# Retention, expert attention and Fourier mixing in one kernel: a load of attention outputs moved three units later, converted weights loaded ahead of others, and one PSUM ring for two phases

## The chip, the cores and the metric

The kernel runs on one core of a Trainium2 chip. The time is the device time of one execution in microseconds (us), and what counts is the median over several executions. The engines are named as in the profile: PE is the matrix engine (TensorE), PEld its weight loads, DVE the vector engine, ACT the scalar engine, POOL the GpSimd engine, and SP the sync engine, which here issues nearly all DMA transfers.

## What is computed

The reference, cut to its three stages (8 batches, 576 positions, 512 features):

```python
# 1. retention, 8 heads of 64: causal, decaying, no softmax
ret = (scale * q @ k.T) * Dmat            # Dmat[i, j] = gamma[h] ** (i - j) for i >= j, else 0
x = (ret @ v)                             # heads side by side: [B, 576, 512]
# 2. attention with 4 experts; the two best experts of each token count
for e in range(4):
    a = softmax(causal(scale * (x @ wq[e]) @ (x @ wk[e]).T))
    ye = a @ (x @ wv[e]) @ wo[e]
    out += gate_weight(x, e) * ye
# 3. mixing over tokens and channels
theta = out @ w_theta
zr, zi = out * cos(theta), out * sin(theta)
u = out + w_tok_r @ zr + w_tok_i @ zi     # over the 576 positions
result = u + relu(u @ w_ch)
```

## The kernel before, in words

**Precision.** Most products are made of three matmuls each: both operands are split into a high and a low part (`split`, lines 105 to 107: the high part is a copy on ACT, the low part a subtraction on DVE), and `mm3` (lines 100 to 103) adds high times high, high times low and low times high. The weights of stage 3 come in 64-bit floats. Conversion jobs (`convert`, lines 460 to 483), spread over phase 1, turn them into high and low halves and put these into DRAM scratch tensors: `TT` for theta, `TD` for the token mixing, `CD` for the channels.

**Phase 1** is a loop over 80 units and one closing step (lines 653 to 727). A unit is (batch, expert pair, block of 128 rows). Step t computes the scores of unit t (`at_scores`), transposes the probabilities of unit t - 1 (`at_trans`), multiplies finished groups with the values (`at_out`), and in between does the retention and the projections of the next batch, by a table (`SLOTS`). The last ten units and the closing step have a table of their own, `LAST` (lines 57 and 58): at t = 70 the second half of the projection for queries (`Q01`) and the first half of the keys of the last pair (`K10`), at 71 `K11`, at 72 `Q10` and the fused product `F0`, at 73 `Q11` and `F1`, and from 74 on nine token tiles of batches 0 and 1 (`T`). In this phase the order of PE is written out by hand; the other engines and the DMA queues follow an order that the planner makes from dependencies and from the program's order.

**The keys** of a projection go out by four DMAs (`KK<-KN`, line 251), which put both heads' halves where the scores want them.

**Towards phase 2**, at the end of t = 69 (lines 706 to 715), `fuse_load` allots staging buffers and loads, in this order, four pieces of the transposed output weights (`wost<-wot`), four pieces of the output weights (`wost<-wo`), and the four converted theta tiles (`th<-tt`, line 523). Then `load_o(0)` and `load_o(1)` load the attention outputs of batches 0 and 1. Each issues five DMAs on SP, one for `ol` (line 575) and four for the gate weights `og` (line 579, one buffer only), and one multiplication `ol * og` on POOL (line 580). `fuse(p)` (lines 532 to 536) multiplies the output weights with theta: 12 matmuls of 512 columns. `token_tile` (lines 585 to 613) makes from a piece of `ol` the features of 128 tokens and their theta: 24 matmuls of 512 columns into two PSUM tiles (`ps` and `th`), emptied by ACT and DVE. Token tile 0 is the first reader of `load_o(0)`; token tile 4, the tile of both batches' last 64 rows, is the first reader of `load_o(1)`.

**Phase 2** (from line 735) goes over the batches. `mix(b, h)` (lines 742 to 803) multiplies the token weights with the modulated features into four accumulators, 108 matmuls, which DVE empties (line 799, for batch 0 line 801); `channel` and `channel2` (lines 808 to 840) multiply with the channel weights into eight tiles, which DVE empties (line 839 or 824). Between the halves of `mix` the token tiles of later batches are made. The order of PE is the planner's too in this phase.

**PSUM.** Phase 1 has a pool `ps1` with a ring of eight banks (`name="w"`, `WB = 8`). It is released ahead of phase 2, and a pool `ps2` takes the same eight banks: four are fixed by name to the accumulators (`acc00` to `acc11`, one buffer each) and four are a ring `w` for token tiles and channel products. Two accumulator sets at the ends (`spare`) take the ring.

Of the kernel before, what the change touches and what calls it, by code (L numbers as in the profile page):

```python
# [10 lines left out]
F32 = mybir.dt.float32  # L11
# [38 lines left out]
WB = 8  # L50
# [13 lines left out]
def tile_kernel(ctx: ExitStack, tc: tile.TileContext, qk, kv, w1, wo, wot, wd, cst, out):  # L64
# [239 lines left out]
    def work(b, names):  # L304
        for n in names.split():
            x = b + n.islower()
            if x < B:
                if n in "Gg":
                    gate(x)
                elif n[0] == "T":  # L310
                    token_tile(ps1, 0, len(X2))
                elif n[0] == "F":
                    fuse(int(n[1]))
                elif n[0] in "Vv":
                    proj_v(x, int(n[1]))
                else:
                    proj_qk(x, int(n[1]), int(n[0] in "Kk"), int(n[2]))
# [188 lines left out]
    def fuse_load():  # L506

        def put(src, sl, h, l):
            st = wa.tile([128, 256], F32, name="wost", bufs=8)
            nc.sync.dma_start(st, src[:, sl])  # L510
            FP.append((h, l, st))

        for kt in range(4):
            wt = wa.tile([128, 2, 2, C], F32R, name=f"wt{kt}", bufs=1)
            put(wot, slice(kt * 256, kt * 256 + 256), wt[:, 0].rearrange("p a c -> p (a c)"),
                wt[:, 1].rearrange("p a c -> p (a c)"))
            FW.append(wt)
        for g in range(4):
            sl = slice((g % 2) * 256, (g % 2) * 256 + 256)
            put(wo, slice(g * 256, g * 256 + 256), WOH[:, g // 2, sl], WOL[:, g // 2, sl])  # L520
        for kt in range(4):
            th = wa.tile([128, 2, DM], F32R, name=f"th{kt}", bufs=1)
            nc.sync.dma_start(th.bitcast(F32), TT[kt])
            FW[kt] = (th, FW[kt])

    def fuse_split(n):
        while FP[n:]:
# [54 lines left out]
            tc.add_manual_dep(m.ins, MARK["ch"].ins.name, mybir.DependencyInfo(  # L582
                mybir.DependencyClass.Sync, mybir.DependencyReason.DATA), reason="behind the channel products")

    def token_tile(pp, g, i):

        b0 = 2 * g
        oh = wk1.tile([128, 2, C], F32R, name="oh", bufs=2)
        ol = wk1.tile([128, 2, C], F32R, name="oll", bufs=2)
        if i == 4:  # L590
            for w in range(2):
                sl = slice(w * 64, w * 64 + 64)
                split(oh[:, :, sl], ol[:, :, sl], OL[b0 + w][:, :, 512:576])
        else:
            b, m = (b0, i) if i < 4 else (b0 + 1, i - 5)
            split(oh, ol, OL[b][:, :, m * C:m * C + C])
        ps = pp.tile([128, DM], F32, name="w", bufs=WB if pp is ps1 else 4)
        for p in range(2):
            mm3(ps, oh[:, p, :], ol[:, p, :], WOH[:, p, :], WOL[:, p, :], p == 0, p == 1)
        if pp is ps1:  # L600
            th = pp.tile([128, DM], F32, name="w", bufs=WB)
        else:
            th = pp.tile([128, DM], F32, name="w", bufs=4)
        for p in range(2):
            mm3(th, oh[:, p, :], ol[:, p, :], MH[:, p, :], ML[:, p, :], p == 0, p == 1)
        x2 = wk1.tile([128, DM], F32, name="x2", bufs=EARLY)
        nc.scalar.activation(x2, ps, AF.Copy)
        k = wk1.tile([128, DM], F32, name="k", bufs=1)
        nc.scalar.activation(k, th, AF.Copy, scale=1.0 / TWO_PI, bias=MAGIC)
        nc.vector.tensor_scalar(k, k, MAGIC, TWO_PI, op0=OP.subtract, op1=OP.mult)  # L610
        nr = wk1.tile([128, DM], F32, name="nr", bufs=EARLY)
        nc.vector.tensor_sub(nr, k, th)
        X2[g, i], NR[g, i] = x2, nr
# [39 lines left out]
    for t in range(nu + 1):  # L653
        b, k = divmod(t, 10)
        if b < B - 1:
            more, between, after = *SLOTS[k], ""
        else:
            b = B - 1
            more, between, after = LAST[t - 10 * b]
        if t < nu:  # L660
            at_scores(units[t])
            work(b, more)
            if units[t][2] == NCH - 1:
                at_norm(*units[t][:2])
        if t == nu - 1:
            assert not jobs[1]
            cvt.release()
            atk.release()
            zp = pool("zp")
        if between == "O":  # L670
            for o in outs:
                at_out(*o)
            outs = []
        ready, new = outs, []
        if t:
            at_trans(units[t - 1])
            ub, up, um = units[t - 1]
            if GROUPS[GRP[um]][-1] == um:
                new.append((ub, up, GRP[um]))
        outs = new  # L680
        if b < B - 1:
            if between[:1] == "R":
                c = int(between[1])
                x = b + 1
                def mid():
                    for o in ready:
                        at_out(*o)

                ret_step(x, c - 1, mid)
            else:  # L690
                outs = ready + outs
        else:
            work(b, between)
            for o in ready if t < nu else ready + outs:
                at_out(*o)
        work(b, after)


        i = int(t >= JOBS[0])
        x = t - JOBS[0] if i else t - 2  # L700
        while jobs[i] and (x + 1) / due[i] >= njobs[i] - len(jobs[i]) + 1 - 1e-6:
            with ExitStack() as es:
                for e in ("dve", "act"):
                    es.enter_context(tc.issue_after(MARK[e].ins))
                jobs[i].pop(0)()
        if t == nu - 11:
            assert not jobs[0]
            ret.release()
            w2 = pool("w2")
            WOH, WOL, MH, ML = [w2.tile([128, 2, DM], F32R, name=x) for x in ("WOH", "WOL", "MH", "ML")]  # L710
            wol = pool("wol")
            wa = pool("wa")
            fuse_load()
            load_o(0)
            load_o(1)
        if t == nu - 10:
            fuse_split(4)
        if t == nu - 8:
            fuse_split(0)
        if t == nu - 7:  # L720
            w1p.release()
            wa.release()
            w2b = pool("w2b")
            TK = w2b.tile([128, 9, 2, S], F32R, name="TK")
            wk1 = pool("wk1")
            for kt in KORD:
                nc.sync.dma_start(TK[:, kt].bitcast(F32), TD[kt])
# [1 line left out]
        z_tile(0, i, 0)  # L729
    first.close()  # L730
    att.release()
    ps1.release()


    wk = pool("wk")
    CH = wk.tile([128, 4, 2, DM], F32R, name="CH")
    for kt in range(4):
        nc.sync.dma_start(CH[:, kt].bitcast(F32), CD[kt])
    ps2 = pool("ps2", space=PSUM)
    UT = {}  # L740

    def mix(b, h, behind=None):
        g, w = divmod(b, 2)
        tiles = [0, 1, 2, 3, 4] if w == 0 else [4, 5, 6, 7, 8]
        ts = TH if b else TS
        spare = h and b in EDGE
        acc = [[ps2.tile([128, t1 - t0], F32, name="w" if spare else f"acc{d}{i}", bufs=4 if spare else 1,
                         padded_shape=[128, 512]) for i, (t0, t1) in enumerate(ts)] for d in range(2)]
        ks = []
        for i in tiles:  # L750
            if w == 0 or i != 4:
# [56 lines left out]
    def channel2(b, ets):  # L808
# [3 lines left out]
        for h in range(2):  # L812
            for et in ets:
                es = slice(et * C, et * C + C)
                for kt in (2 * h, 2 * h + 1):
                    for j, (t0, t1) in enumerate(TH):
                        if not kt:
                            ps[et, j] = ps2.tile([128, t1 - t0], F32, name=f"acc{et % 2}{j}", bufs=1,
                                                 padded_shape=[128, 512])
                        mm3(ps[et, j], CH[:, kt, 0, es], CH[:, kt, 1, es], uh[:, kt, t0:t1], ul[:, kt, t0:t1],  # L820
                            kt == 0, kt == 3)
                for j, (t0, t1) in enumerate(TH if h else []):
                    o = u[:, et, t0:t1]
                    MARK["ch"] = nc.vector.scalar_tensor_tensor(o, ps[et, j], 0.0, o, op0=OP.max, op1=OP.add)
                    if b == B - 1:
                        nc.sync.dma_start(out[b, et, :, t0:t1], o)
                if h and b < B - 1:
                    nc.sync.dma_start(out[b, et], u[:, et, :])

    def channel(b, et):  # L830
# [1 line left out]
        u = XU[b]  # L832
        es = slice(et * C, et * C + C)
        for j, (t0, t1) in enumerate(TH):
            ps = ps2.tile([128, t1 - t0], F32, name="w", bufs=4, padded_shape=[128, 512])
            for kt in range(4):
                mm3(ps, CH[:, kt, 0, es], CH[:, kt, 1, es], uh[:, kt, t0:t1], ul[:, kt, t0:t1], kt == 0, kt == 3)
            o = u[:, et, t0:t1]
# [30 lines left out]
    for b in range(B):  # L869
# [6 lines left out]
        mix(b, 0)  # L876
        for x in q[:2]:
            if x not in X2:
                token_tile(ps2, *x)
            if b:  # L880
                x_put(*x)
        def put():
# [5 lines left out]
        mix(b, 1, None if b else put)  # L888
        for x in q[2:]:
            if x not in X2:  # L890
                token_tile(ps2, *x)
            if b:
                x_put(*x)
        if 0 < b < B - 1:
# [4 lines left out]
            continue  # L899
        for i in range(2):  # L900
            channel2(b, (2 * i, 2 * i + 1))
    ps2.release()
    wk.release()
    zp.release()
    wk1.release()
# [79 lines left out]
```

## Time and profile before

| | us |
|---|---|
| median of 3 runs | 880.44 |
| lowest and highest | 877.99 and 881.26 |
| profiled execution, its own time | 879.58 |
| its span (first to last instruction) | 877.8 |
| PE busy in the span | 859.2 |

The profile is one execution, taken by the hardware profiler. In a timeline a line has start, duration, engine, line of the kernel, operation, tiles (written <- read), the shape and how many instructions were merged into it; in brackets stands the idle time of the engine before it and what ended it. In a list of waits the numbers are the total in us, how often, and the longest. Matmuls overlap one another, so what PE loses at a place is better read from starts than from the idle time in brackets.

### The profile page before, as it was taken

The numbers are of one execution on the slowest core, as the hardware profiler recorded it, in microseconds if no ns is written. First come the engines' busy times: TensorE is split into PE (matmuls) and PEld (weight loads), VectorE is DVE, ScalarE is ACT, GpSimd is POOL, SyncE is SP. The second block draws the span as 40 slices with busy tenths as digits, with TensorE's granted clock in tenths as the row PEclk, the third lists the DMA queues.
The fourth block names the chain that finished last, engine by engine and source line by source line (L and its number), as shares of the span: only waits on it lengthen the run. The fifth ranks groups of instructions, "written<-read, shape, count | busy, mean of one in ns | idle before, by whom it ended". The sixth has DMA issues, their size and how long they took to land.

```text
span 877.8 us, 25574 instructions
## 1 busy us (share of the span) xinstructions
PE 859.2 (98%) x10072; PEld 795.2 (91%) x10072; DVE 622.0 (71%) x1729; ACT 454.6 (52%) x1258; POOL 218.7 (25%) x268
## 2 busy tenths in 40 slices
PE   6999999999999999999999999999999999999998
PEld 6989889888888989898789999999989999999998
DVE  4588787878788886876678777676377665766632
ACT  1366667666666766666576445353244533444320
POOL 3325253443525453341300012010210103001010
PEclk9899999999999999999999999999999999999999
DMA  9857677676867676548674442422525233241411
GB/s 317 246 155 239 171 221 199 194 224 187 255 169 222 202 211 179 160 108 238 185 265 170 83 111 47 120 37 61 141 57 139 62 96 93 34 124 25 100 34 54
DMA packets 140440, 130.30 MB, mean 148 GB/s; under 512 B 75808, under 2 KB 114976, under 8 KB 140320
## 3 DMA queue, kind: packets, MB, share of 16 engines
q1 hardware_dynamic: 140176, 128.39, 52.6%
q8 instruction: 79, 1.29, 0.6%
q0 software_dynamic: 144, 0.28, 0.2%
q14 instruction: 41, 0.34, 0.1%
HBM read 78.03 MB, written 32.00 MB: 125 GB/s over the span
## 4 chain that ended last, share of the span: by engine, by line
PE 88%; DMA 4%; DVE 3%; ACT 1%; issue 1%; POOL 1%; SPq 0%; ACTq 0%; DVEq 0%; POOLq 0%
PE acc L787 22%; PE w L245 11%; PE w L101 6%; PE w L102 6%; PE w L103 6%; PE w L335 6%; PE w L273 6%; PE w L401 5%; PE w L382 5%; PE w L787 3%; PE w L158 3%; PE w L143 3%; DMA kt<-qk 2%; DMA KK<-KN 1%; PE w L180 1%
## 5 line engine op out<-in xcount | busy, mean ns | idle before, releaser
L787 PE MATMUL acc<-TK,zh 128*128 128x288 f32 (+2 forms) x896 | 156.4, 296 | 0.5 <-ACT ob L405 0.5
L787 PEld LDWEIGHTS acc<-TK,zh 128*128 128x128 f32 x896 | 132.1, 189 | 1.2 <-issue 0.6
L343 ACT ACTIVATE P<-P,st 128x128 f32<-128x128 f32 (+4 forms) x160 | 95.4, 598 | 42.2 <-DVE st L338 41.9
L803 POOL TENSOR_TENSOR ul<-u,uh 128x576 fp32r<-128x576 f32 x16 | 24.2, 1531 | 309.6 <-ACT uh L802 309.6
L787 PE MATMUL acc<-TK,zl 128*128 128x288 f32 (+1 forms) x448 | 95.9, 295 | 0.0
L106 ACT ACTIVATE zh<-cs 128x512 fp32r<-128x512 f32 x64 | 40.3, 630 | 76.6 <-PE acc L787 61.4
L335 PE MATMUL w<-KK,U 128*64 128x288 f32 (+4 forms) x384 | 76.6, 327 | 1.5 <-DMA KK<-KN 1.4
L107 DVE TENSOR_TENSOR zl<-cs,zh 128x512 fp32r<-128x512 f32 x64 | 45.1, 705 | 43.2 <-ACT zh L106 42.5
L338 DVE CUSTOM_DVE_ANT_0 P<-w,cm 128x128 f32<-128x128 f32 (+4 forms) x160 | 71.1, 477 | 4.8 <-PE w L335 3.9
L787 PEld LDWEIGHTS acc<-TK,zl 128*128 128x128 f32 x448 | 72.4, 189 | 0.0
L626 ACT ACTIVATE cs<-cs,quarter 128x256 f32<-128x256 f32 x72 | 36.5, 507 | 55.4 <-DVE cs L624 55.2
L629 DVE SCALAR_TENSOR_TENSOR cs<-cs,x 128x512 f32<-128x512 f32 x72 | 50.7, 706 | 20.1 <-ACT cs L627 19.4
L382 PE MATMUL w<-ident,P 128*128 128x128 f32 (+2 forms) x480 | 60.1, 260 | 1.6 <-DVE sm L147 1.3
L335 PEld LDWEIGHTS w<-KK,U 128*128 128x128 f32 (+1 forms) x384 | 54.0, 171 | 8.0 <-DVE nwt L355 1.5
L193 POOL TENSOR_TENSOR xl<-xt,xh 128x512 fp32r<-128x512 f32 (+1 forms) x40 | 47.8, 1195 | 45.4 <-ACT xh L192 45.4
L479 POOL TENSOR_TENSOR r<-r,ex 128x192 f32<-128x192 f32 (+1 forms) x51 | 29.5, 578 | 116.2 <-ACT hl L480 42.0
L192 ACT ACTIVATE xh<-xt 128x512 fp32r<-128x512 f32 (+1 forms) x40 | 23.5, 589 | 66.9 <-DVE xt L190 66.8
L103 PE MATMUL w<-uh,CH 128*128 128x288 f32 x192 | 56.6, 295 | 0.0
L102 PE MATMUL w<-ul,CH 128*128 128x288 f32 x192 | 56.5, 294 | 0.0
L101 PE MATMUL w<-uh,CH 128*128 128x288 f32 x192 | 56.5, 294 | 0.0
L401 PE MATMUL w<-PT,V 128*64 128x192 f32 (+3 forms) x576 | 56.4, 325 | 0.0
L382 PEld LDWEIGHTS w<-ident,P 128*128 128x128 f32 (+2 forms) x480 | 47.1, 138 | 8.3 <-DVE sm L147 2.7
(153 smaller groups left out, 2340.4 us busy)
## 6 DMA issues: line engine op xcount, KB each, us to landing
KK<-KN SPq DMA_DIRECT2D x128, 144.0 KB
kt<-qk SPq DMA_DIRECT2D x32, 512.0 KB
kv<-kv SPq DMA_DIRECT2D x32, 512.0 KB
raw<-wd SPq DMA_DIRECT2D x43, 192.0 KB
xd<-xb SPq DMA_DIRECT2D x126, 64.0 KB
out<-u SPq DMA_DIRECT2D x28, 288.0 KB
u<-xd SPq DMA_DIRECT2D x28, 288.0 KB
td<-hl SPq DMA_DIRECT2D x27, 192.0 KB
```

The source lines that it names most:

```text
L101: nc.tensor.matmul(ps, ah, bh, start=first, stop=False)
L102: nc.tensor.matmul(ps, ah, bl, start=False, stop=False)
L103: nc.tensor.matmul(ps, al, bh, start=False, stop=last)
L245: nc.tensor.matmul(ps, W[:, kt, w0:w0 + 128], x[:, kt, sl], start=x is xh and W is WH and kt == 0, stop=x is xl and kt == 3)
L273: nc.tensor.matmul(ps[:R], x[:, kt, cs], W[:, kt, w0:w0 + NV], start=x is xh and W is WH and kt == 0, stop=x is xl and kt == 3)
L335: nc.tensor.matmul(ps[s][:R], U[:, s, rs], KK[:, s, x, j0:j1], start=x == 0, stop=x == 1)
L338: MARK["dve"] = nc.vector.tensor_tensor_reduce(Ps[s][:R, j0:j1], ps[s][:R], cm[:R, o + j0:o + j1], 1.0, st[:R, 0, s:s + 1] if i else 3.0e3 ...
L343: MARK["act"] = nc.scalar.activation(Ps[s][:R, :n], Ps[s][:R, :n], AF.Exp, bias=st[:R, last, s:s + 1], scale=-1.0, accum_out=SUM[p][:R, m, ...
L382: nc.tensor.transpose(tp[:w, j, :], Ps[s][:R, j * C:j * C + w], ident[:R, :R])
L401: nc.tensor.matmul(po[s * 64:s * 64 + 64, c0:], V[:ROWS[j], j, 2 * p + s, :], v, start=j == 0, stop=j == last, skip_group_check=True)
L629: nc.vector.scalar_tensor_tensor(z, cs, -1.0, x2[:, None, ds].to_broadcast([128, 2, 256]), op0=OP.mult, op1=OP.mult)
L787: nc.tensor.matmul(acc[d][j], A[:, dc], TK[:, kt, W, t0:t1], start=q == 0 and n == 0, stop=q == 8 and n == 2)
```

## The change

Three things change. In `fuse_load` the four loads of converted theta tiles stand ahead of the four loads of the output weights (the transposed ones stay first). `load_o(1)` leaves the end of t = 69 and stands at the end of t = 72, behind `fuse_split(0)`. And the pool `ps1` with its ring of eight banks lives on through phase 2: all accumulators, channel products and token tiles take the next place of that one ring, and `ps2`, its fixed accumulators and the special cases go.

```diff
@@ fuse_load
-        for g in range(4):
-            sl = slice((g % 2) * 256, (g % 2) * 256 + 256)
-            put(wo, slice(g * 256, g * 256 + 256), WOH[:, g // 2, sl], WOL[:, g // 2, sl])
         for kt in range(4):
             th = wa.tile([128, 2, DM], F32R, name=f"th{kt}", bufs=1)
             nc.sync.dma_start(th.bitcast(F32), TT[kt])
             FW[kt] = (th, FW[kt])
+        for g in range(4):
+            sl = slice((g % 2) * 256, (g % 2) * 256 + 256)
+            put(wo, slice(g * 256, g * 256 + 256), WOH[:, g // 2, sl], WOL[:, g // 2, sl])
@@ token_tile: the pool is no longer an argument
-        ps = pp.tile([128, DM], F32, name="w", bufs=WB if pp is ps1 else 4)
+        ps = ps1.tile([128, DM], F32, name="w", bufs=WB)
...
-        if pp is ps1:
-            th = pp.tile([128, DM], F32, name="w", bufs=WB)
-        else:
-            th = pp.tile([128, DM], F32, name="w", bufs=4)
+        th = ps1.tile([128, DM], F32, name="w", bufs=WB)
@@ the loop over units
             fuse_load()
             load_o(0)
-            load_o(1)
         if t == nu - 10:
             fuse_split(4)
         if t == nu - 8:
             fuse_split(0)
+            load_o(1)
@@ between the phases
-    ps1.release()
...
-    ps2 = pool("ps2", space=PSUM)
@@ mix
-        spare = h and b in EDGE
-        acc = [[ps2.tile([128, t1 - t0], F32, name="w" if spare else f"acc{d}{i}", bufs=4 if spare else 1,
-                         padded_shape=[128, 512]) for i, (t0, t1) in enumerate(ts)] for d in range(2)]
+        acc = [[ps1.tile([128, t1 - t0], F32, name="w", bufs=WB, padded_shape=[128, 512]) for t0, t1 in ts]
+               for d in range(2)]
@@ channel2
-                            ps[et, j] = ps2.tile([128, t1 - t0], F32, name=f"acc{et % 2}{j}", bufs=1,
-                                                 padded_shape=[128, 512])
+                            ps[et, j] = ps1.tile([128, t1 - t0], F32, name="w", bufs=WB, padded_shape=[128, 512])
@@ channel
-            ps = ps2.tile([128, t1 - t0], F32, name="w", bufs=4, padded_shape=[128, 512])
+            ps = ps1.tile([128, t1 - t0], F32, name="w", bufs=WB, padded_shape=[128, 512])
@@ the end
-    ps2.release()
+    ps1.release()
```

## Rows read from the trace of the kernel before

**Rows 1.** The page: the span, and PE's share of it (busy us, instructions).

```profile
span 877.8 us, 25574 instructions
...
PE 859.2 (98%) x10072; PEld 795.2 (91%) x10072; DVE 622.0 (71%) x1729; ACT 454.6 (52%) x1258; POOL 218.7 (25%) x268
```

**Rows 2.** Who waited for whom, PE: us in total, times, longest us.

```profile
PE w L335 <- DMA KK<-KN: 1.4, 1, 1.4
...
PE w L101 <- DMA th<-tt: 0.8, 2, 0.5
...
PE w L101 <- ACT oh L106: 0.7, 1, 0.7
...
PE acc L787 <- ACT ob L405: 0.5, 1, 0.5
PE acc L787 <- DVE u L799: 0.3, 1, 0.3
```

**Rows 3.** Timeline of PE: starts and followers of the two fused products.

```profile
409.22 0.48 PE L101 MATMUL w<-th,wt 128*128 128x512 f32 x1
...
413.56 0.44 PE L401 MATMUL w<-PT,V 128*64 128x128 f32 x4
...
417.13 0.48 PE L101 MATMUL w<-th,wt 128*128 128x512 f32 x1
...
419.97 1.22 PE L335 MATMUL w<-KK,U 128*64 128x288 f32 x8
```

**Rows 4.** Timeline of PE: two score steps over 128 columns and their followers.

```profile
397.73 0.64 PE L335 MATMUL w<-KK,U 128*128 128x128 f32 x4
398.20 0.74 PE L245 MATMUL w<-xh,WH 128*128 128x288 f32 x4
...
426.20 0.44 PE L335 MATMUL w<-KK,U 128*128 128x128 f32 x2
...
428.26 0.45 PE L101 MATMUL w<-WOH,oh 128*128 128x512 f32 x1
```

**Rows 5.** Timelines of PE and DVE where phase 2 begins.

```profile
461.38 1.78 PE L401 MATMUL w<-PT,V 128*64 128x192 f32 x20
463.66 0.89 PE L787 MATMUL acc<-TK,zh 128*128 128x256 f32 x5 [0.49 <-ACT ob L405]
...
463.19 0.69 DVE L107 TENSOR_TENSOR zl<-cs,zh 128x512 fp32r<-128x512 f32 x1
```

**Rows 6.** Timeline of SP (DMA issues): the loads around the change.

```profile
394.77 0.90 SPq L510 DMA_DIRECT2D wost<-wo  x2
...
403.04 2.69 SPq L523 DMA_DIRECT2D th<-tt  x4
...
411.23 2.05 SPq L251 DMA_DIRECT2D KK<-KN  x2
421.51 2.40 SPq L579 DMA_DIRECT2D og<-gd  x4
423.95 3.96 SPq L251 DMA_DIRECT2D KK<-KN  x6
```

**Rows 7.** Timeline of POOL: the multiplications of the two loads.

```profile
418.80 2.68 POOL L580 TENSOR_TENSOR ol<-ol,og 128x1152 f32<-128x1152 f32 x1 [11.15 <-DMA KK<-KN]
426.93 2.64 POOL L580 TENSOR_TENSOR ol<-ol,og 128x1152 f32<-128x1152 f32 x1 [5.45 <-DMA og<-gd]
```

**Rows 8.** Timeline of PE: first matmuls of token tiles 0 and 4.

```profile
421.98 0.50 PE L101 MATMUL w<-WOH,oh 128*128 128x512 f32 x1
...
440.83 0.39 PE L101 MATMUL w<-WOH,oh 128*128 128x512 f32 x1
```

**Rows 9.** Timeline of DVE: a step of token tile 0.

```profile
427.81 2.03 DVE L610 TENSOR_SCALAR k<-k 128x512 f32<-128x512 f32 x1 [0.56 <-ACT k L609]
```

**Rows 10.** Phase 2, PE's second mixing half of batch 1, and DVE's emptying in batch 3.

```profile
533.43 0.54 PE L787 MATMUL acc<-TK,zth 128*128 128x288 f32 x2 [0.28 <-DVE u L799]
...
629.73 1.62 DVE L799 TENSOR_TENSOR u<-acc,u 128x288 f32<-128x288 f32 x4 [1.18 <-PE acc L787]
```

More of the change, by code (lines that the diff above doesn't have):

```diff
@@ L310, in work @@
                 elif n[0] == "T":
-                    token_tile(ps1, 0, len(X2))
+                    token_tile(0, len(X2))
                 elif n[0] == "F":
@@ L583, in load_o, with token_tile @@
                 mybir.DependencyClass.Sync, mybir.DependencyReason.DATA), reason="behind the channel products")
-    def token_tile(pp, g, i):
+    def token_tile(g, i):
         b0 = 2 * g
@@ L878, in tile_kernel @@
             if x not in X2:
-                token_tile(ps2, *x)
+                token_tile(*x)
             if b:
@@ L890, in tile_kernel @@
             if x not in X2:
-                token_tile(ps2, *x)
+                token_tile(*x)
             if b:
```

## The prediction, made before the changed kernel was run

> **What bounds the kernel now.** I read four views, in this order. First the page: PE is busy for 859.2 of 877.8 us [rows 1], so no other engine sets the time over any long stretch, and a change that leaves the matmuls alone, as this one does, can win only what PE spends waiting, 18.6 us in all. Second, PE's list of waits, to see which of these waits the edits touch [rows 2]. Four do belong to them: the wait for key copies (1.4), two waits for theta tiles (0.8), one wait at the first mixing step for ACT's emptying of the last phase-1 bank (0.5), and one wait for DVE's emptying of an accumulator (0.3). Together 3.0 us of idle time: the size of what can happen is a third of a per cent. Third, PE's timeline at each of these places, since a matmul that restarts is longer than one in a run and the loss is more than the idle time. Fourth, SP's and POOL's timelines, for what holds the late transfers.
>
> The reader should see a chain there. SP issues its DMAs in order. It issued two of the four key copies of `K10` at 411.23, and then the gate-weight loads of `load_o(1)` stood at its head; they had to wait, for `og` has one buffer and the first `load_o` multiplies out of it until 418.80 + 2.68 = 421.48. Only at 421.51 did SP go on, and the other two copies of `K10`, with the four of `K11`, went out from 423.95 on [rows 6, 7]. PE did the first two score matmuls at 426.20 and then had to wait [rows 4].
>
> **The change part by part.**
>
> *Theta tiles ahead of output weights.* The fused product F0 takes from 409.22 to 413.56, 4.34 us; F1, the same 12 matmuls with everything there, takes from 417.13 to 419.97, 2.84 us [rows 3]. So the late tiles cost 1.50 us. In the new order the first two theta tiles go out where two pieces of output weights went, at 394.77, and the other two right behind the key and gate transfers, before 403.04 [rows 6]: over 8 us and over 2 us earlier for the last two than they have to be to save 1.5. Gain taken: 1.50, between 0.8 (the idle time alone, [rows 2]) and 1.50. The price is that the output weights come some 2 us later, by their exchange of places with the rest of the theta loads, 2.69 us of issue for four [rows 6]. Their splits feed ACT and DVE at t = 72 and their first reader on PE is token tile 0, at 421.98 [rows 8], some 16 us behind the end of these issues at 405.73. I cost it at nothing; if the cover is gone, ACT's work behind a late split moves by the same 2 us at most.
>
> *`load_o(1)` three units later.* What moves are five DMA issues on SP (four of them 2.40 us together) and one POOL multiplication of 2.64 us [rows 6, 7]. On SP they go behind all eight key copies of `K10` and `K11`, which is the point: the copies of `K10` then follow one another from 411.23 on and land well ahead of PE, and nothing stands behind a waiting `og` load but later work. The score step cost 2.06 us from 426.20 to 428.26; the same step over 128 columns took 0.47 us at 397.73 [rows 4]. Gain 1.59, between 1.4 (the idle time, [rows 2]) and 1.59. The queue is also lighter: without the second `ol` (576 KB by its shape) ahead of the key copies, and with theta gone earlier, the four `og` loads of `load_o(0)` land earlier, and so does its multiplication. That is needed, for token tile 0 starts at 421.98, half a microsecond behind the multiplication's end at 421.48 [rows 7, 8]: if PE comes 1.5 us earlier and the multiplication does not, the first gain is lost at this place. I expect the multiplication some 3 us earlier, because two theta tiles of four, 512 KB each by their shape, are out of its way. What is late next is the second multiplication. Its reader is token tile 4, at 440.83, and by then it has been done since 429.57 [rows 7, 8]; with PE 3.1 us earlier, 8 us of cover are left, more than the three units can eat as long as `og` is waited for only until the first multiplication. On POOL it is moved past conversion work whose results are wanted in phase 2 only: nothing.
>
> *One ring.* At the hand-over the first accumulator waits for ACT to empty the very last phase-1 tile, idle 0.49 [rows 5], since the new pool begins when all of the old one is done. In one ring the accumulators take banks used some tiles before. But PE would then be there at 463.17, and the low part of the first modulated tile ends at 463.19 + 0.69 = 463.88 [rows 5]; four matmuls of high parts come first (of the five in 0.89 us), so about 0.2 of the 0.49 comes back as a wait for DVE. Gain 0.30, between 0.1 and 0.49. In phase 2 the accumulators are no longer fixed by name: the second half of batch 1 has not to wait for the emptying of the first half if four other banks are free, and the idle 0.28 [rows 10] goes: 0.28, between a loss of as much and 0.28. All other crossings in phase 2 show no idle time before, so the ring can win nothing there; what it may lose is the second rival.
>
> Sum: 1.50 + 1.59 + 0.30 + 0.28 = 3.67 us. On the profiled execution's own time, 879.58 (span 877.8 and 1.8 around it), that gives 875.9; the median of the runs shown is 0.86 above that execution, so for a median 880.44 - 3.67 = 876.8, 0.42% less.
>
> *A row against the moved load.* While POOL multiplied from 426.93 to 429.57, DVE's step on token tile 0 took 2.03 us, and it ended at 429.84, just behind POOL [rows 7, 9]. So a DVE instruction that meets this multiplication can last until it is over. The multiplication moves, and it will meet other DVE work; PE's part in it is the third rival. The Trainium skill has this as a rule (SBUF — State Buffer, "Who interferes with whom"): GpSimd and certain vector instructions take the same pair of ports as an exclusive lock, and the one that starts later is held until the first is over. By that rule the moved load would cost the length of one multiplication wherever PE waits for the DVE step that meets it; the trace agrees in that the DVE step ended 0.27 us behind POOL.
>
> **The rivals.**
>
> *One more stall goes.* PE also waits 0.7 us for a split at a token tile of phase 2 [rows 2]. With free banks in any place the planner can order PE's work otherwise and keep it busy there. For: the planner moves whole blocks when a bank is not free. Against: that split waits for a load, not for a bank. Time: 880.44 - 3.67 - 0.7 = 876.1, and a little less where restarts count.
>
> *Reused banks are the freshest.* If the ring hands the next user the bank that was emptied last, PE stands at each crossing from `mix` to the work behind it until DVE has emptied four accumulators, 1.62 us [rows 10], where fixed names gave it other banks. Eight batches have seven such crossings with other work between the halves: 7 x 1.62 = 11.3 us. Against the 3.4 us won elsewhere this ends at 880.44 - 3.4 + 11.3 = 888.3, slower. One bank instead of four, 0.41 each, costs 2.8 and ends at 879.9; slower by over 0.5% needs at least 7.8 us, so it decides from about 1.1 us a crossing. For: nothing in the trace of before shows which bank a shared ring gives. Against: phase 1 works with such a ring of eight, and its waits for banks in the list are small.
>
> *A cover is too short.* Token tile 0 finds the first multiplication undone, or a DVE step that PE waits for meets the second one. The first takes back at most 1.50, the second at most 2.03 [rows 9]: 878.3 to 878.8.
>
> *The move does nothing.* The planner may issue the moved loads as early as before, since they depend on little. If the `og` loads still stand between the key copies, the 1.59 stay lost: 878.4. Against: what stands earlier in the program has gone first on SP whenever it was ready.
>
> **How the numbers follow.** About 0.5%, 4.4 us, is what a measurement of this kernel can tell from no change, that is a time below 876.0 or above 884.8. Forecast as summed 0.52; one more stall goes 0.18; a cover too short 0.14; the move does nothing 0.08; freshest banks 0.08. The forecast, 876.8, is near the bound, and the bounds of its terms (2.0 to 3.9 us) with restarts and the scatter of medians put about 0.15 of its 0.52 below 876.0; with the first rival's 0.18 this makes faster 0.33. Slower is the second rival less its cheap end, 0.07. The rest, 0.60, is within 0.5%. The range leaves out most of the second rival, and on the low side what is more than 3 us beyond the forecast: 873.8 to 880.2.
>
> **What would show it.** In the profile of the changed kernel F0 should take 2.8 us, the score step over 128 columns ahead of token tile 1 about 0.5 us, and SP should show eight key copies without a stop. PE's list of waits should have no line with `th` or `KK`, and the first mixing matmul should wait for DVE's `zl`, if for anything. A wait of PE at token tile 0 for `oh`, or at a crossing in phase 2 for line 799, 839 or 607, would show the cover or the ring to be wrong. The prediction is wrong if PE's total idle time falls by less than 2 us or by more than 6, or if PE's busy time changes with the same matmuls.

## The result: slower by 1%, lost at one place that the prediction had not read

The changed kernel takes 888.10 us (median of 4 executions, 886.92 to 890.84); the kernel before, in the same comparison, 879.22 (4 executions, 876.63 to 881.26). The ratio is 1.0105, 95% interval 1.0076 to 1.0135. Forecast were 876.8 us, a gain, and a range of 873.8 to 880.2: the time lies above the range, and the sign is wrong too.

The page of the kernel after, first its span and busy times, then two rows of its 40 slices, each of 22 us:

```profile
span 886.5 us, 25575 instructions
...
PE 859.4 (97%) x10072; PEld 795.9 (90%) x10072; DVE 623.5 (70%) x1729; ACT 455.9 (51%) x1258; POOL 219.9 (25%) x268
...
PE   7899999999999999999999999999699999999998
...
PEclk9999999999999999999999999999799999999999
```

PE is busy for as long as in [rows 1], with as many matmuls. What grew is its idle time, 886.5 - 859.4 = 27.1 us where 18.6 stood before. One slice, the 29th (620.6 to 642.7 us), falls to 6 tenths and takes the granted clock down with it. PE's list of waits says what it is:

```profile
PE w L101 <- ACT oh L106: 8.5, 1, 8.5
```

The 0.7 us of the same line in [rows 2] have become 8.5. The lines for `KK`, `th`, `ob` at line 787 and the accumulators, the other four of [rows 2], are gone from the list. So all three parts of the change took away what they were to take away, and something else costs more. PE's timeline says where (lines 781, 793 and 797 of the kernel after are lines 787, 799 and 803 of the one before):

```profile
411.44 0.48 PE L101 MATMUL w<-th,wt 128*128 128x512 f32 x1
...
414.37 0.44 PE L401 MATMUL w<-PT,V 128*64 128x128 f32 x4
...
426.78 0.66 PE L335 MATMUL w<-KK,U 128*128 128x128 f32 x4
427.28 0.44 PE L101 MATMUL w<-WOH,oh 128*128 128x512 f32 x1
...
460.41 1.78 PE L401 MATMUL w<-PT,V 128*64 128x192 f32 x20
462.12 1.33 PE L781 MATMUL w<-TK,zh 128*128 128x256 f32 x8
...
628.32 0.43 PE L781 MATMUL w<-TK,zl 128*128 128x288 f32 x2
637.27 0.80 PE L101 MATMUL w<-WOH,oh 128*128 128x512 f32 x1 [8.52 <-ACT oh L106]
...
642.10 0.40 PE L103 MATMUL w<-MH,oll 128*128 128x512 f32 x1
```

The first three pairs answer to [rows 3], [rows 4] and [rows 5]: F0 takes 414.37 - 411.44 = 2.93 us (4.34 before), the score step 0.50 (2.06), the hand-over 1.71 (2.28). The fourth is the loss: the last matmul of the first mixing half of batch 3 starts at 628.45, and the first matmul of the next token tile (the first of batch 4) at 637.27.

With starts of PE at four places the whole execution divides into stages. F0 is the first fused product; mix(0,0) the first matmul of phase 2; mix(3,0) the first half of the mixing of batch 3; ch(3) its channel products. The table has the profiled execution of every kernel of this study (e1 to e10 are below; "ring" is the shared ring of eight banks):

| us | start of F0 | F0 to mix(0,0) | mix(0,0) to mix(3,0) | mix(3,0) to ch(3) | ch(3) to last matmul |
|---|---|---|---|---|---|
| before | 409.22 | 54.44 | 152.41 | 43.44 | 214.17 |
| **after** | 411.44 | 50.68 | 152.07 | **53.47** | 214.17 |
| e1, both moves, no ring | 409.17 | 51.24 | 152.72 | 43.41 | 214.17 |
| e2, ring alone | 407.70 | 54.05 | 152.07 | 53.82 | 214.17 |
| e3, ring, `ul` on DVE | 409.88 | 50.68 | 152.34 | 49.88 | 214.17 |
| e4, ring, tiles later | 410.95 | 50.68 | 152.08 | 42.43 | 214.26 |
| e5, theta alone | 408.66 | 51.59 | 152.73 | 43.44 | 214.17 |
| e6, `load_o(1)` alone | 409.82 | 51.88 | 152.39 | 43.41 | 214.17 |
| e7, ring, input later | 409.74 | 50.68 | 152.38 | 57.41 | 214.17 |
| e8, no ring, input later | 413.43 | 51.24 | 153.01 | 43.85 | 214.29 |
| e9, as e4 | 409.34 | 50.68 | 152.07 | 42.42 | 214.52 |
| e10, no ring, tiles later | 408.66 | 51.31 | 152.97 | 42.40 | 214.37 |

From before to after that is -3.76, -0.34, +10.03 and 0.00, in sum +5.9. The other 2.7 of the 8.65 by which the spans differ are 2.22 at the start, ahead of anything that the change touches there, and 0.5 behind the last matmul. The start of F0 scatters from 407.70 to 413.43 over the kernels of the table (e2 with the ring has the earliest, e8 without it the latest), so I take the 2.22 for scatter of single executions. That isn't shown, and the medians leave it open: they differ by 8.9 us (6.7 to 11.9 by the interval), more than the 5.9 of the stages, and in e3, e4 and e9, which have all three parts of the change too, the medians also lie some 2 us higher against before than the stages behind F0 say (in e7 0.4).

Why PE stands there is told by the chain of waits of the kernel after, from 619.95 on (start, length, engine and line on the chain; "issue" is time in which the engine waited for nothing that the profile shows):

```profile
619.95 8.55 PE w L781 x64
...
628.52 0.64 ACT zh L106
...
629.79 0.83 DVE u L793 x2
...
630.69 0.69 ACT uh L796
...
631.45 0.66 POOL ul L797
...
634.21 2.58 POOL ol L580
...
636.80 0.42 ACT oh L106
...
637.27 0.80 PE w L101
```

The token tile needs `oh`, the high part of `ol`, and `ol` is ready when POOL has multiplied it by the gate weights (line 580). On POOL that multiplication stands behind two subtractions `ul` of batch 3. These need `uh` from ACT, which needs `u`, which DVE makes when the first mixing half is done (and, here, behind a split `zh`, `zl` for the next half). So the token tile behind this half waits, through four engines, for the end of this very half: 8.8 us from start to start, with PE empty.

The chain was there before as well. The timelines of POOL and of PE of the kernel before:

```profile
631.68 2.94 POOL L803 TENSOR_TENSOR ul<-u,uh 128x576 fp32r<-128x576 f32 x2 [41.85 <-ACT uh L802]
634.58 2.67 POOL L580 TENSOR_TENSOR ol<-ol,og 128x1152 f32<-128x1152 f32 x1
```

```profile
636.59 0.42 PE L787 MATMUL acc<-TK,zl 128*128 128x288 f32 x2
637.74 0.50 PE L101 MATMUL w<-WOH,oh 128*128 128x512 f32 x1 [0.73 <-ACT oh L106]
```

POOL ends at 637.25 here too. But PE did other work meanwhile: its mixing matmuls run on from 616.07 to 636.72, 156 of them, where a half has 108. The planner had put 48 matmuls of the *second* half, 6.4 us at 0.133, ahead of the token tile; only 0.7 us of the wait were left. In the kernel after it goes 108, 24, 108, 36: half, two token tiles, half, three token tiles, which is the program's order. (A token tile is 12 matmuls of 512 columns, six into `ps` and six into `th`, not 24 as the section on the kernel says.) The ring took away the work that had covered the chain.

The chain itself also became longer. Counted from the start of the half, POOL ends after 637.25 - 616.07 = 21.2 us before and 636.78 - 614.19 = 22.6 us after. The timeline of DVE of the kernel after:

```profile
629.18 0.69 DVE L107 TENSOR_TENSOR zl<-cs,zh 128x512 fp32r<-128x512 f32 x1 [2.51 <-ACT zh L106]
629.79 1.54 DVE L793 TENSOR_TENSOR u<-w,u 128x288 f32<-128x288 f32 x4
```

The split `zl` of the next half stands ahead of the four emptyings `u`; in the kernel before, `u` went first, at 629.73 [rows 10], and this `zl` at 631.27. So of the 7.8 us that PE stands longer (8.7 against 0.9, from starts), 6.4 are the missing 48 matmuls and 1.4 the longer chain.

Only batch 3 pays. Batches 1 and 5 issue the same pair of loads, but in the kernel after POOL multiplies the first of them at 507.38 and 733.54, ahead of `ul` and 13 us ahead of the token tiles at 520.91 and 747.21. Why the planner put batch 4's multiplication behind `ul`, in both kernels, isn't settled.

### The profile page after: what moved, and what is told of

Its sections match the earlier page's. It is cut to its first block, busy times and chain, and to the rows that moved or that the text cites. A ratio compares the mean times of both kernels' runs of the same rounds, so it can differ in the third digit from the quotient of the medians.

```text
span 886.5 us, 25575 instructions
## 1 busy us (share of the span) xinstructions
PE 859.4 (97%) x10072; PEld 795.9 (90%) x10072; DVE 623.5 (70%) x1729; ACT 455.9 (51%) x1258; POOL 219.9 (25%) x268
## 4 chain that ended last, share of the span: by engine, by line
PE 88%; DVE 4%; DMA 3%; issue 2%; POOL 1%; ACT 1%; SPq 0%; DVEq 0%; ACTq 0%; POOLq 0%
PE w L781 26%; PE w L245 11%; PE w L101 8%; PE w L102 8%; PE w L103 8%; PE w L335 6%; PE w L401 5%; PE w L382 5%; PE w L273 5%; PE w L158 3%; PE w L143 2%; DMA kt<-qk 2%; PE w L180 1%; PE w L173 1%; DMA raw<-wd 1%
## 5 line engine op out<-in xcount | busy, mean ns | idle before, releaser
L781 PE MATMUL w<-TK,zh 128*128 128x288 f32 (+2 forms) x1024 | 178.6, 296 | 0.1
L781 PEld LDWEIGHTS w<-TK,zh 128*128 128x128 f32 x1024 | 150.8, 189 | 0.6 <-DVE u L793 0.3
L781 PE MATMUL w<-TK,zl 128*128 128x288 f32 (+2 forms) x512 | 109.4, 295 | 0.0
L781 PEld LDWEIGHTS w<-TK,zl 128*128 128x128 f32 x512 | 82.9, 189 | 0.0
L103 PE MATMUL w<-uh,CH 128*128 128x288 f32 x256 | 75.4, 295 | 0.0
L101 PE MATMUL w<-uh,CH 128*128 128x288 f32 x256 | 75.4, 295 | 0.0
L102 PE MATMUL w<-ul,CH 128*128 128x288 f32 x256 | 75.4, 295 | 0.0
```

The lines of the kernel that those rows point to most:

```text
L101: nc.tensor.matmul(ps, ah, bh, start=first, stop=False)
L102: nc.tensor.matmul(ps, ah, bl, start=False, stop=False)
L103: nc.tensor.matmul(ps, al, bh, start=False, stop=last)
L781: nc.tensor.matmul(acc[d][j], A[:, dc], TK[:, kt, W, t0:t1], start=q == 0 and n == 0, stop=q == 8 and n == 2)
```

## The experiments

The theories that I set out with: **A**, the ring alone makes the loss, by the order of PE at this one place; **B**, the moved `load_o(1)` makes it, by what it shifts on SP and POOL; **C**, the prediction's slow rival, that the ring hands out freshly emptied banks and each crossing loses a little. For e7 and e8: **P**, one ring shared by accumulators and token tiles keeps PE in the program's order, so nothing can be pulled ahead; **Q**, the planner chose that order for a reason that has nothing to do with the sharing.

### e1: both moves without the ring

```diff
 fuse_load: th<-tt stands ahead of wost<-wo, as in the change
 t == nu - 12:   -            load_o(1)
 t == nu - 8:    +            load_o(1)
```

> The kernel before with the two moved loads and without the one ring. Theory A (the ring alone makes the loss; the moves win what was forecast): some 3.1 us under the kernel before, about 876, both phase-1 waits of PE gone (F0 near 2.9 us, score step near 0.5 us), and PE's wait at the token tile of phase 2 stays near 0.7 us. Theory B (the moved load shifts the order of POOL and SP behind it and so makes the wait in phase 2): PE waits some 8 us for the split of that token tile here too, time 885 or more.

877.35 us (10 executions), 0.9985 of before (0.9967 to 1.0003; before 879.41 in 20). F0 to mix(0,0) falls from 54.44 to 51.24, mix(3,0) to ch(3) stays at 43.41. In its list of waits the lines for `KK` and `th` are gone; the one for `ob` at the hand-over (0.5), which the ring took away, stays, and the one for `oh` at the token tile has the 0.7 us of before. So the moves don't make the loss, against B. What they win shows in the stages (3.2 us up to mix(0,0)); the medians differ by 2.1 us, less than the 3.1 expected, with an interval that takes in no change.

### e2: the ring without the moves

```diff
-    ps1.release()
-    ps2 = pool("ps2", space=PSUM)
+    acc, channel products and token tiles: ps1.tile(..., name="w", bufs=WB)
 loads in the order of before
```

> The one ring alone, loads as in the kernel before. Theory A: PE waits some 8 to 9 us at the first token tile of batch 4, as in the changed kernel, then runs some 10 matmuls at half pace, and with 0.5 to 1 us won at the beginning of phase 2 and in batch 1 the time is 9 to 10 us over the kernel before, 888 to 890; both phase-1 waits are as before. Theory B: no such wait, 878 to 879.

888.82 us (4), 1.0130 of before (1.0104 to 1.0156). Its list of waits has the late loads of before (`KK` 1.4, `th` 1.2) and the stall of after (`oh` 8.5, once) side by side. The ring makes all of the loss: 53.82 us from mix(3,0) to ch(3), and no other stage is longer than before. The time is in the range of A, 888 to 890. A holds so far, and B is out.

### e5 and e6: each move alone

e5 has the new order of theta and output weights only, e6 only `load_o(1)` three units later.

> The kernel before with the theta loads moved ahead and nothing else. If the terms of the sum stand by themselves: F0 takes 2.9 us instead of 4.3, and the score step ahead of token tile 1 still waits for key copies, 2.0 us. If the two gains hang together (token tile 0 stands until the first multiplication of attention outputs is done, as the second load is still in the queue), PE waits some 1 us at token tile 0. No new wait in phase 2.

> The kernel before with the load of batch 1's attention outputs moved and nothing else. F0 still takes some 4.3 us, as theta comes as late as before; the score step takes 0.5 us instead of 2.1. No new wait in phase 2: its wait at the token tile stays near 0.7 us. Theory B (the moved load makes the wait in phase 2) would want 8 us there.

One execution each, 876.46 and 877.55 us (before 880.09 in 9). A single time says little here, since those of before in this comparison run from 875.98 to 882.63; the stages say more. F0 to mix(0,0) gains 2.85 with e5 and 2.56 with e6, together 5.41, where both moves in one kernel (e1) gain 3.20. The gains overlap, against the expectation that each term stands by itself. PE's wait for `oh` at the token tile of phase 2 is 0.7 us in both, against B. The timelines of PE and of POOL of e5:

```profile
411.58 0.44 PE L401 MATMUL w<-PT,V 128*64 128x128 f32 x4
...
424.62 0.41 PE L335 MATMUL w<-KK,U 128*128 128x128 f32 x2 [0.18 <-DMA KK<-KN]
424.87 0.45 PE L101 MATMUL w<-WOH,oh 128*128 128x512 f32 x1
```

```profile
415.44 2.67 POOL L580 TENSOR_TENSOR ol<-ol,og 128x1152 f32<-128x1152 f32 x1 [8.34 <-PE w L382]
```

With theta out of the way the first multiplication starts 6.78 us behind F0's start (408.66), where [rows 3, 7] give 9.58. `og` is free that much earlier, and the key copies behind it come in time for all but 0.18 us: the score step, which began at 424.00, takes 0.87 us instead of 2.06, though `load_o(1)` has not moved. The other way round, PE's timeline in e6:

```profile
409.82 0.48 PE L101 MATMUL w<-th,wt 128*128 128x512 f32 x1
...
412.49 0.50 PE L101 MATMUL w<-th,wt 128*128 128x512 f32 x1 [0.33 <-DMA th<-tt]
413.38 0.44 PE L401 MATMUL w<-PT,V 128*64 128x128 f32 x4
```

Without the second load in the queue F0 takes 3.56 us instead of 4.34, though theta has not moved.

### e3: the subtractions of batch 3 off POOL

```diff
-            MARK["u"] = (nc.vector if h else nc.gpsimd).tensor_sub(ul[:, k, :], u[:, k, :], uh[:, k, :])
+            MARK["u"] = (nc.vector if h or b == 3 else nc.gpsimd).tensor_sub(ul[:, k, :], u[:, k, :], uh[:, k, :])
```

> The changed kernel, but in batch 3 the low parts of u in the first half are made by DVE, not by POOL, so that the POOL multiplication for batch 4 has no work of that batch ahead of it. Theory A (PE stands at the token tile since its input's multiplication is queued on POOL behind the low parts): the wait of 8.5 us goes, 10 us less than the changed kernel, 876 to 878. Theory C (the loss is spread over the crossings of phase 2, as the ring gives banks that were just emptied): no more than 1 us less, 887. If the loads of batch 4 themselves are late, the wait stays in part and shows DMA as its releaser.

884.11 us (5), 1.0083 (1.0056 to 1.0110), and the stall still has 5.6 us. The timelines of PE, POOL, ACT and DVE of e3:

```profile
633.08 0.79 PE L101 MATMUL w<-WOH,oh 128*128 128x512 f32 x1 [5.62 <-ACT oh L106]
```

```profile
619.42 2.68 POOL L580 TENSOR_TENSOR ol<-ol,og 128x1152 f32<-128x1152 f32 x1 [32.74 <-DVE cs L621]
...
627.39 2.61 POOL L580 TENSOR_TENSOR ol<-ol,og 128x1152 f32<-128x1152 f32 x1 [5.29 <-DMA og<-gd]
```

```profile
631.36 1.36 ACT L796 ACTIVATE uh<-u 128x576 fp32r<-128x576 f32 x2 [3.50 <-DVE u L793]
632.63 0.70 ACT L106 ACTIVATE oh<-ol 128x256 fp32r<-128x256 f32 x2
```

```profile
627.89 2.65 DVE L107 TENSOR_TENSOR zl<-cs,zh 128x512 fp32r<-128x512 f32 x1 [2.07 <-ACT zh L106]
```

I had expected POOL to be the only link, and that was wrong. The time came down by 4 us and not by the 10 expected. The multiplication is done at 622.10, long ahead, but on ACT the split `oh` stands behind `uh`, which waits for the same end of the mixing half. Besides, the edit brought POOL's next multiplication up against this end: DVE's `zl` met it and took 2.65 us, and `u` started 3.3 us behind the half's last matmul (627.16 to 630.46), where it was 1.3 in the kernel after. That is some 2 of the 5.6 us. The order around this half is written into more than one queue; whoever takes out one link meets the next.

### e4 and e9: the token tiles behind the second half, with the ring

```diff
-        for x in q[:2]:
+        for x in q[:0 if b == 3 else 2]:
...
-        for x in q[2:]:
+        for x in q[0 if b == 3 else 2:]:
```

This is the kernel after with the first two token tiles of batch 3's turn put, in the program itself, behind the second mixing half. e9 is the same kernel with more executions.

> The changed kernel with the first two token tiles of batch 3 written behind the second mixing half instead of between the halves. Theory A: PE has 108 matmuls, 14.4 us, to do while POOL works, the 8.5 us and the half pace go, 876 to 878. Theory C: a crossing more or less changes nothing, 886 to 888. A new wait of up to 2 us for the emptying of the first half's accumulators is possible, since the ring then has both halves next to each other.

> The changed kernel with the first two token tiles of batch 3 written behind the second mixing half, as run before, in more rounds. If the three gains of the change stand (3.7 us in phase 1, 0.4 in batch 1) and the order alone was at fault, it is 3.5 to 5 us under the kernel before, 0.4 to 0.55%, with an interval clear of no change. It should be 1 us under the next kernel.

876.44 us (10), 0.9978 (0.9952 to 1.0004), and 875.76 us (12), 0.9966 (0.9947 to 0.9985; before 878.62 in 23). Only e9's interval is clear of no change; its gain, 2.9 us, is less than the 3.5 to 5 expected. The timelines of PE and of POOL of e4:

```profile
642.24 0.43 PE L781 MATMUL w<-TK,zl 128*128 128x288 f32 x2
642.51 0.39 PE L101 MATMUL w<-WOH,oh 128*128 128x512 f32 x1
```

```profile
633.74 2.67 POOL L580 TENSOR_TENSOR ol<-ol,og 128x1152 f32<-128x1152 f32 x1
```

POOL's multiplication ends at 633.74 + 2.67 = 636.41, 22.7 us behind the start of the half (22.6 in the kernel after), but PE comes to the tile 6 us behind it, without a gap: 216 mixing matmuls, then 60 of the tiles. With one order restored in one batch all of the loss is gone (42.43 us from mix(3,0) to ch(3), 1.0 less than before), while every bank still comes from the ring. That refutes C, by which this edit should have given back about a seventh.

### e7 and e8: the same input, three copies later

To tell P from Q, both kernels have three copies of `ol` onto itself (values unchanged) on POOL, behind the multiplication for batch 4: e7 with the ring, e8 is e1 with them. If the planner's order on PE answers to when the input comes, a later input should bring more matmuls ahead of the tile.

```diff
+        for _ in range(3 if b == 4 else 0):
+            m = nc.gpsimd.tensor_copy(OL[b], OL[b])
```

> The changed kernel with three copies of the attention outputs of batch 4 onto themselves on POOL behind their multiplication, so that the token tile's input is some 5 to 8 us later (the values stay). Theory P (in one ring the planner gives banks in the program's order, so the second mixing half cannot start ahead of the token tiles in front of it): PE's wait grows by as much, to 13 to 17 us, and the time to 893 to 897. Theory Q (the planner had other reasons, and puts the second half first when the token tile is late enough): the wait falls below 2 us and the time to 876 to 880.

> The same three copies in the kernel with the moved loads and fixed accumulators (no ring). Theory P: the planner fills the time with more matmuls of the second mixing half, PE's wait at the token tile stays below 3 us, the time within 3 us of the kernel with the moved loads alone, 876 to 880. Theory Q makes no difference between this kernel and the one with the ring.

e7 takes 890.64 us (2; 1.0145, 1.0078 to 1.0212), e8 878.07 (8; 0.9979, 0.9960 to 0.9997; before 880.09). The timelines of POOL and of PE of e7, then of PE of e8:

```profile
635.43 3.56 POOL L582 COPY ol<-ol 128x1152 f32<-128x1152 f32 x3
```

```profile
639.50 0.80 PE L101 MATMUL w<-WOH,oh 128*128 128x512 f32 x1 [12.14 <-ACT oh L106]
```

```profile
643.00 0.50 PE L101 MATMUL w<-WOH,oh 128*128 128x512 f32 x1 [1.17 <-ACT oh L106]
```

With the ring PE keeps its order and the 3.56 us of copies come on top in full: 12.1 us of idle time against 8.5. That is below the 13 to 17 us and 893 to 897 expected under P, as the copies are shorter than the 5 to 8 us taken for them. With the fixed accumulators the planner pulls 72 matmuls of the second half ahead instead of 48 (180 mixing matmuls stand before the tile, from 617.68 to 641.54), and the wait grows by only half a microsecond. This supports P: with fixed accumulators the order follows the input, with the ring it didn't, at either of the two delays. The other batches agree. In batch 1 the program has two token tiles between the halves, 24 matmuls: in all six kernels with the ring PE does these 24 there, in all six without it the planner pulls two more tiles ahead, and it is 48 (before, from 522.08 to the second half at 533.43; after, from 520.91 to 526.38). What rule of the planner makes it so stays inferred from its orders; two separate rings, one for the accumulators and one for the rest, were not run.

### e10: the token tiles behind the second half, without the ring

e1 with the edit of e4.

> The kernel with the moved loads and fixed accumulators, no ring, and the same order of token tiles in batch 3. It has the gains of the moved loads (3.1 us) and loses the 0.7 us of idle time and the restart at the token tile of batch 4 (1.1 us), but keeps the waits at the hand-over and in batch 1 (1 us together): 3.5 to 4.5 us under the kernel before. If the ring itself won nothing, it equals the kernel with the ring and this order.

875.84 us (12), 0.9964 (0.9947 to 0.9981), beside e9's 875.76. Both beat the kernel before and the changed one, and these times don't tell them apart. Its gain on the kernel before, 2.8 us, is less than the 3.5 to 4.5 expected, and e9 is not the 1 us faster that was expected of it. In the stages e9 is ahead by 0.63 us up to mix(0,0) and by 0.90 from there to mix(3,0), and behind by 0.15 at the end: some 1.4 us that the ring wins in one profile each; the waits at the hand-over and for accumulators (0.5 and 0.6 us in e10's list) are missing in e9's. The medians of 12 executions, each scattering over 5 us or more, don't show it.

## Why the prediction was wrong

**The moved loads: right in the stages.** Of its sum of 3.67, the 1.50 for theta came as 4.34 - 2.93 = 1.41, and the 1.59 for the key copies as 2.06 - 0.50 = 1.56. The cover that I had worried about held: the first multiplication starts 7.07 us behind F0's start instead of 9.58, 2.5 earlier where I had expected some 3, and ends at 421.20, 1.4 us ahead of token tile 0. The second ends at 435.24, 4.6 us ahead of token tile 4 (439.85), where 8 us of cover were forecast. The timelines of SP and of POOL of the kernel after:

```profile
397.00 0.43 SPq L520 DMA_DIRECT2D th<-tt  x1
403.99 1.51 SPq L520 DMA_DIRECT2D th<-tt  x3
...
412.94 6.49 SPq L251 DMA_DIRECT2D KK<-KN  x8
422.77 2.41 SPq L579 DMA_DIRECT2D og<-gd  x4
```

```profile
418.51 2.69 POOL L580 TENSOR_TENSOR ol<-ol,og 128x1152 f32<-128x1152 f32 x1 [8.62 <-DMA KK<-KN]
...
432.56 2.68 POOL L580 TENSOR_TENSOR ol<-ol,og 128x1152 f32<-128x1152 f32 x1 [0.24 <-DMA og<-gd]
```

The eight key copies go out in a row, as was said, and the `og` loads behind them. One detail was off: the theta tiles went one and three, not two and two. The two gains were summed as if each needed its own move; the sum held in the stages, but e5 and e6 show that either move alone brings 2.6 to 2.9 of the 3.2 us that both bring up to mix(0,0).

**The hand-over: better than forecast.** I took 0.30 and expected a wait for `zl`; the stretch became 0.57 shorter and no such wait appeared. The timelines of PE and of DVE of the kernel after say why:

```profile
463.29 0.70 PE L781 MATMUL w<-TK,zl 128*128 128x256 f32 x4
```

```profile
462.21 0.68 DVE L107 TENSOR_TENSOR zl<-cs,zh 128x512 fp32r<-128x512 f32 x1
```

Eight matmuls of the high part go first (from 462.12, shown above), not four, and `zl` is done at 462.89, before its first reader at 463.29. The 0.28 of batch 1 came as well, as far as single executions show it: 0.34 between mix(0,0) and mix(3,0), where the kernels with the ring differ among themselves by 0.31, and the line for the accumulators is gone.

**The crossings: the step that failed.** It read: "All other crossings in phase 2 show no idle time before, so the ring can win nothing there; what it may lose is the second rival." A crossing without idle time is one that something covers, and I didn't ask what. The front section says that the order of PE in phase 2 is the planner's; the prediction treated that order as given for the forecast and as more free in its first rival ("with free banks in any place the planner can order PE's work otherwise"). The ring did the reverse. With its own four banks the second half could go ahead of a token tile that was late; in one ring it stayed in the program's order. The price of that one place is 8.7 us of standing (637.27 - 628.45, less one pitch of 0.13) and 2.3 of slow restart (last section), less the 1.0 lost there before (0.9 of standing, 0.1 of restart): the 10.0 of the stages, two and a half times what all the other stages won.

The row that should have led there was among mine: the 0.7 us of `oh` at a token tile [rows 2]. I wrote of it that "that split waits for a load, not for a bank". It waits for POOL's multiplication, queued behind `ul`, and what stood in front of it on PE were 48 matmuls of the next half. A look at the 48 matmuls in front of this tile would have raised the question of what let them go ahead; that it was the separate accumulators is shown only by e2, e4, e7 and e8.

**The slow rival: the number, not the mechanism.** Freshest banks were priced at 7 x 1.62 = 11.3 us and gave 888.3; measured are 888.10. That is a coincidence. By that rival seven crossings lose 1.62 us each; in the trace six lose nothing (three lie ahead of mix(3,0), a stage 0.34 shorter, and three behind ch(3), 214.17 us in both kernels) and one loses ten, and e4 wins it all back with every bank still from the one ring.

**The other rivals.** "One more stall goes" pointed at the right stall with the wrong sign. "A cover is too short" and "the move does nothing" didn't happen: DVE met the second multiplication, but in conversion work that PE doesn't wait for:

```profile
433.25 2.07 DVE L470 TENSOR_SCALAR b<-raw 128x128 int32<-128x128 int32 x1
```

The same step on the same shape took 0.22 us at 354.92. This one ends at 435.32, 0.08 us behind POOL's 432.56 + 2.68. The Trainium skill's rule (SBUF — State Buffer, "Who interferes with whom"), that the later of the two is held until the first is over, agrees with this row. In e3 such a meeting reaches the path: `zl` took 2.65 us instead of 0.69 while POOL's next multiplication ran from 627.39 to 630.00, and held up the emptying of the mixing half behind it.

## What to carry to other kernels

Where a planner orders an engine's work, separate buffers can also be its freedom to run ahead, as in this kernel: before merging two rings into one, look at each place where work of one stands in front of a late piece of the other, and price that place as if the order became the program's. A crossing without idle time isn't a crossing without a chain; follow the chain of the next consumer through the other queues and count what covers it. And if an order is worth something, write it into the program, as e4 and e10 do, since then it doesn't hang on how buffers are allotted.

## What the hardware showed that I had not expected

**The restart after the stall.** These are windows of the kernel after (from and to, length, busy time of PE, weight loads, DVE, ACT and POOL with their instructions, granted clock, DMA share, GB/s):

```profile
628.00:637.00 9.00, 0.75 (x6) 0.51 (x4) 2.15 (x5) 2.19 (x4) 5.32 (x3) 0.71 0.00 0
637.00:642.00 5.00, 4.73 (x11) 3.76 (x12) 1.47 (x3) 1.12 (x3) 0.00 (x0) 0.50 0.37 121
642.00:660.00 18.00, 18.00 (x125) 17.29 (x125) 10.73 (x19) 5.49 (x12) 2.68 (x1) 1.00 0.30 63
```

While PE stood for 8.5 us the granted clock fell, and from 637 to 642 it was at 0.50, the lower level of 1.2 GHz. From 637.27 to 642.10 eleven matmuls of 512 columns took 4.83 us, nearly all at a pitch of 0.43 where it is 0.23 at 2.4 GHz: 4.83 - 11 x 0.23 = 2.3 us on top of the wait. Behind the 0.73 us of before and the 1.17 of e8 the tile's matmuls went on at 0.23 from the second on; behind the 5.62 us of e3 the pitch was 0.43 too.

**How little a copy costs on POOL.** In e7 three copies of 128x1152 onto themselves took 3.56 us, 1.2 each, where a multiplication of that shape takes 2.6 to 2.7.
